# Scores of batches 3 to 7 moved into the slot ahead, in front of a double group of state products, with the PSUM banks passed on

## The chip, the cores and the metric

One core of a Trainium2 chip. TensorE (PE) multiplies matrices into PSUM, ScalarE (ACT) and VectorE (DVE) do elementwise work and empty PSUM, GpSimd (POOL) and SyncE (SP) issue most of the DMAs. The time is device microseconds of one execution of the whole kernel; lower is better.

## The reference, cut to what matters

There are 8 batches and 8 heads; x is 512 x 64 and state 32 x 64 per head. Attention runs both ways, then follow two feed-forward nets over 4352 rows (8 batches of 512 x rows and 32 state rows).

```python
scores = scale * x @ state.T             # softmax -> a;  xread = a @ state
scores2 = scale * state @ x.T            # softmax -> a2; sread = a2 @ x
h = relu(cat(xread, sread) @ w_in); y = (h * h) @ w_out
out = ((y @ w1) * (y @ w2)) @ w3 @ w_out2
```

`scores` is `scores2` transposed, so the kernel computes one of them and turns it.

## The kernel before, in words

**Stage 1, up to about 600 us, is the one that the change touches.** It computes the attention and the first feed-forward net together, for one batch c at a time, in slots. A slot i is one entry (c, f) of the list `order`: f is one of 16 blocks of 128 columns of w_in. From slot 48 on, c = i // 16 and f = i % 16; batch 2's first half, and the second halves of batches 0 to 2, stand in slots 16 to 47.

`h_tile` (L477) computes h for the slot: six full-array matmuls (L485) in fp32r, high and low words, into a bank of tag `h`. It doesn't multiply xread by w_in: as xread is a @ state, it multiplies a by the product of state and w_in, which `make_sw` has made. `act_h` (L469) then runs on ACT a Relu out of the bank (L471), a Square (L473) and the cast to the high half of `ghl` (L81), and on DVE the subtraction that gives the low half (L82). `y_tile` (L513) multiplies `ghl` by w_out with 12 full-array matmuls (L524), up to two slots later.

`make_sw` (L449) makes the state products SW of a batch and one group of four blocks: 8 matmuls in f32, each on a tile of 64 rows x 32 columns of the array, which run as 16 instructions (L454) into two banks, one per row half r. Each bank is then split: a cast on ACT (L81, `sw`) and a subtraction on DVE (L82, `sw`). `sw_pair` (L641) makes two groups one after the other, the first in the two banks of tag `m`, the second in the two of tag `h`. Pairs stand in the slots 15, 23, 31, ..., 119, directly behind the slot's `h_tile`; then follow two y tiles (24 matmuls) and no other work of TensorE.

`scores` (L315) makes the scores of one batch: 8 matmuls of the same shape as those of a state group, 16 instructions (L320), into the two `m` banks, and copies each bank to an SBUF tile `S` with ACT (L327). I call the copy of bank r S0 or S1. From `S` follow the softmax steps: `soft2` reads S directly, `soft1a` turns it on DVE (for batches from 3 on).

**PSUM** has eight banks: two `m`, two `h` and four `y`.

**What sets the order.** Lists by slot name the work beside `h_tile` and `y_tile`: `side` (behind `h_tile` and the pair) and `late` (behind `y_tile`), both kept behind an earlier slot's ghl subtraction. For batch b from 3 to 7 (BLK is 3) `att_slots` gives the attention steps for the slots from (b - 1) * 16 on, and the scores are the first of them, in slot (b - 1) * 16: 32, 48, 64, 80 and 96. Their input xT is turned on DVE (`turn_x`, L275) in slots (b - 2) * 16 + 10 and + 11. In slots 15 to 30 `conv` (L624) converts one weight block per slot; of a block of w_out, the split into high and low words (`wo`) is traced by the next slot's `conv`.

The program's order is a priority only. A planner that knows each operation's cost lays out the order of every engine ahead of the run: when an engine is free in its plan, it takes the first operation in program order that it thinks is ready, and a later one where the earlier isn't. On the chip each engine then works through its instructions in that fixed order.

**Stage 2** (from about 600 us) multiplies w3 by w_out2 and computes the second net from y. The change does not touch it.

Of the kernel before, what the change touches and what calls it, by code (L numbers as in the profile page):

```python
# [20 lines left out]
def kernel(  # L21
# [17 lines left out]
    nc = tc.nc  # L39
# [10 lines left out]
    NF = DF // P  # L50
# [6 lines left out]
    BLK = 3  # L57
# [13 lines left out]
    def bank_m(name):  # L71
        return psum.tile([P, 512], F32, tag="m", bufs=2, name=name)

    def bank_h(name):
        return psum.tile([P, 512], F32, tag="h", bufs=2, name=name)
# [4 lines left out]
    def split(hi, lo, src):  # L80
        nc.scalar.copy(hi, src)  # L81
        return nc.vector.tensor_tensor(out=lo, in0=src, in1=f32(hi), op=ALU.subtract)  # L82
# [212 lines left out]
    def att_steps(b):  # L295
# [19 lines left out]
        def scores():  # L315
            pss = [bank_m("ps_s") for _ in range(G)]
            for k in range(HG):
                for r in range(G):
                    rows = slice(r * D, (r + 1) * D)
                    nc.tensor.matmul(  # L320
                        pss[r][k * NS:(k + 1) * NS, :], stT[rows, b, k, :], xT[b, k][rows, :],
                        start=True, stop=True, tile_position=(r * D, k * NS),
                    )
            for r in range(G):
                pool, tag, bufs = (att, "S", 2) if b else (wpool, "wo", NF)
                s = pool.tile([P, 512], F32, tag=tag, bufs=bufs, name="S")
                last = nc.scalar.copy(s, pss[r])  # L327
                v["S", r] = s
            return last

# [92 lines left out]
            sread, sread_T,  # L423
        )

    def att_slots(b):
        if b >= B:
            return [[] for _ in range(NF)]
        xp, sc, s2, s1a, s1b, at, a2t, sr, srt = att_steps(b)
        if b > BLK:  # L430
            return [
                [sc], [], [s2[0], s1a[0]], [],
                [s1b[0], s2[1]], [a2t[0]], [at[0], s1a[1]], [a2t[1]],
                [s1b[1]], [sr], [at[1]], [srt], [], [], [], [],
            ]
        if b == BLK:
            return [
                [sc], [], [s2[0], s1a[0]], [], [s1b[0], s2[1]], [a2t[0]], [], [a2t[1]],
                [at[0], s1a[1]], [sr], [s1b[1]], [srt], [at[1]], [], [], [],
            ]  # L440
        return [
            [xp[0]], [xp[1]], [xp[2]], [xp[3]], [sc], [s1a[0]], [s1b[0]], [at[0], s1a[1]],
            [s1b[1]], [at[1]], [s2[0]], [a2t[0], s2[1]], [], [a2t[1]], [sr], [srt],
        ]
# [4 lines left out]
    def make_sw(b, fg, cols=slice(0, 512), banks=None):  # L449
        pss = [banks(r, "ps_sw") if banks else bank_m("ps_sw") for r in range(G)]  # L450
        for k in range(HG):
            for r in range(G):
                rows = slice(r * D, (r + 1) * D)
                mm = nc.tensor.matmul(  # L454
                    pss[r][k * NS:(k + 1) * NS, cols], stT[rows, b, k, :], win_t[fg][rows, k, cols],
                    start=True, stop=True, tile_position=(r * D, k * NS),
                )
        last_sw.append(mm)
        for r in range(G):
            if (b, fg, r) not in SW:  # L460
                SW[b, fg, r] = pa.tile([P, 2, 512], F32R, tag=f"sw{r}", bufs=2, name=f"sw{r}")
            t = SW[b, fg, r]
            split(t[:, HI, cols], t[:, LO, cols], pss[r][:, cols])
# [13 lines left out]
    def h_tile(c, f):  # L477
        ph = bank_h(f"ph{c}_{f}_")
        if c < B:
            fg, m = f // 4, f % 4  # L480
            k = 0
            for g in range(G):
                s, a = SW[c, fg, g], aT_t[c, g]
                for wi, ai in PASSES:
                    mm = nc.tensor.matmul(  # L485
                        ph, s[:, wi, m * P:(m + 1) * P], a[:, ai, :],
                        start=(k == 0), stop=(k == 3 * G - 1),
                    )
                    k += 1
            h_mms.append(mm)  # L490
            act_h(c, f, ph, 512)
        else:
            cols = slice((f % 4) * P, (f % 4 + 1) * P)
            t = pa.tile([P, 2, ND, P], F32R, tag=f"sw{f % 2}", bufs=2, name="w9")
            split(t[:, HI], t[:, LO], win_t[f // 4][:, :, cols])
            for k in range(ND):
                for i, (wi, xi) in enumerate(PASSES):
                    nc.tensor.matmul(
                        ph[:, :NT9], t[:, wi, k, :], x9_t[k // 2][:, xi, k % 2, :],
                        start=(k == 0 and i == 0), stop=(k == ND - 1 and i == 2),  # L500
                    )
            act_h(c, f, ph, NT9)
# [3 lines left out]
    def split_x9(g):  # L506
        t = pa.tile([P, 2, 2, NT9], F32R, tag=f"aT{g}", bufs=2, name="x9")
        split(t[:, HI], t[:, LO], x9T[:, 2 * g:2 * g + 2, :])
        x9_t.append(t)
# [3 lines left out]
    def y_tile(c, f):  # L513
        n = 512 if c < B else NT9
        part, (f0, f1) = [(i, sg) for i, sg in enumerate(segs[c]) if sg[0] <= f < sg[1]][0]
        if f == f0:
            for d in range(ND):
                y_ps[c, d] = bank_y(d, f"y{d}")
        if wo_t[f] is None:
            close_splits()  # L520
        t = g_t.pop((c, f))
        for d in range(ND):
            for k, (wi, gi) in enumerate(PASSES):
                nc.tensor.matmul(  # L524
                    y_ps[c, d][:, :n], wo_t[f][:, wi, d * P:(d + 1) * P], t[:, gi, :n],
                    start=(f == f0 and k == 0), stop=(f == f1 - 1 and k == 2),
                )
            if f == f1 - 1:
                pool, tag = (pa, "yo") if d < 2 or c >= B - 1 else (att, "yo2")
                o = pool.tile([P, 512], F32, tag=tag, bufs=2, name="yo")  # L530
                if d % 2 and c > 1:
                    nc.vector.tensor_copy(o[:, :n], y_ps[c, d][:, :n])
                else:
                    nc.scalar.copy(o[:, :n], y_ps[c, d][:, :n])
                nc.sync.dma_start(y_scr[c][part][:, d, :], o[:, :n])
# [49 lines left out]
    xp, sc, s2, s1a, s1b, at, a2t, sr, srt = att_steps(0)  # L585
# [12 lines left out]
    last = s1b[1]()  # L598
# [39 lines left out]
    def sw(b, fg):  # L638
        return lambda: make_sw(b, fg)

    def sw_pair(b, fg):  # L641
        make_sw(b, fg)
        make_sw(b, fg + 1, banks=lambda r, name: bank_h(name))

    side = {i: [] for i in range(NF * B)}
    late = {}
# [21 lines left out]
    pairs = {15: (2, 0), 23: (0, 2), 31: (1, 2), 39: (2, 2), 47: (3, 0)}  # L668
# [9 lines left out]
    for b in range(BLK, B):  # L678
        for i, steps in enumerate(att_slots(b)):
            late[(b - 1) * NF + i] = steps  # L680
        for g in range(G):
            i = (b - 2) * NF + 12 + g
# [17 lines left out]
    def load_wo2(i):  # L700
        t = stage["wo2", i] = w34p.tile([P, 2, 512], F32, tag="wst2", bufs=4, name="wst2")
        rows = wo2_s.rearrange("(a k p) e -> a p k e", a=4, p=NS)
        for a in range(4):
            nc.sync.dma_start(t[a * NS:(a + 1) * NS], rows[a, :, 2 * i:2 * i + 2, :])

    def split_wo2(j):
        t = w34p.tile([P, 2, DM], F32R, tag="wo2", bufs=N1, name="wo2")
        split(t[:, HI], t[:, LO], stage["wo2", j // 2][:, j % 2])
        wo2_t[j] = t

    def load_w3(kk):
        load_stage(("w3", kk), w3_s[:, 4 * kk:4 * kk + 4].rearrange("p (h d) c -> p h (d c)", h=2))
# [4 lines left out]
    for i, (c, f) in enumerate(order):  # L717
        h_tile(c, f)
        if i in pairs:
            sw_pair(*pairs[i])  # L720

        gate = done[i - 3] if i >= 8 else first
        with tc.issue_after(gate.ins):
            for job in side.get(i, ()):
                job()
        if c == B - 1 and f == 11:
            att_cm.__exit__(None, None, None)
            w34_cm = tc.tile_pool(name="w34p", bufs=1, reuse_waits="tile")
            w34p = w34_cm.__enter__()
            for j in range(N1 // 2):  # L730
                load_wo2(j)
        if c == B - 1 and f == NF - 1:
            split_x9(0)
            split_x9(1)
        if c == B:
            if f < N1:
                split_wo2(f)
            if f in (2, 4, 6, 8):
                load_w3(N1 // 2 + f // 2 - 1)
        pend.append((c, f))  # L740
        while len(pend) > (1 if i in pairs else 2):
            y_tile(*pend.pop(0))
        with tc.issue_after(done[i - 3].ins) if i >= 8 else nullcontext():
            for job in late.get(i, ()):
                job()
# [480 lines left out]
    for s, todo in enumerate((turns, turns[::-1])):  # L1226
# [9 lines left out]
        for i, (c0, c1) in enumerate(todo):  # L1236
            for m in range(QM):
                last = quad(c0, c1, m)
# [46 lines left out]
```

## Time and profile before

| | us |
|---|---|
| median of 3 runs | 1220.3 (1218.64 to 1220.49) |
| the profiled execution's own time | 1219.03 |
| its span | 1217.3 |
| PE busy in it | 1201.4 |
| DVE busy | 869.4 |
| ACT busy | 662.2 |

The span runs from the first to the last instruction of the profiled execution; its own time has 1.7 us around that. Busy time of an engine is the time in which at least one of its instructions ran. In a timeline a row merges neighbouring instructions of one kind: start, how long from the first start to the last end, and the count. Instructions on one engine overlap a little: the next starts before the one ahead has ended, so the step from start to start is what an instruction costs its engine. What stands in brackets is idle time ahead of the row and what ended it.

### The profile page before, as it was taken

How to read it: one execution, taken by the hardware profiler on the slowest of the kernel's cores; microseconds unless marked ns; L12 is line 12 of the kernel's file. 1: busy time of each engine (PE TensorE's matmuls, PEld its weight loads, DVE VectorE, ACT ScalarE, POOL GpSimd, SP SyncE). 2: the span in 40 equal slices, each digit the busy share in tenths (PEclk: the TensorE clock that was granted, in tenths of full speed). 3: DMA queues.
4: the chain of work that ended last, by engine and by line, in shares of the span. 5: the costliest groups of instructions: out<-in, count | busy, mean ns of one | idle time of the engine just before them, and what ended most of it. 6: DMA issues, size and time to landing. Idle time of an engine off the chain costs nothing.

```text
span 1217.3 us, 18891 instructions
## 1 busy us (share of the span) xinstructions
PE 1201.4 (99%) x7174; PEld 999.6 (82%) x7174; DVE 869.4 (71%) x1594; ACT 662.2 (54%) x1220; POOL 109.4 (9%) x163
## 2 busy tenths in 40 slices
PE   7999999999999999999999999999999999999998
PEld 5677777777778777778899888989898989898988
DVE  6968877677586766742435875878696957877877
ACT  6877466555464655654656653546363635453542
POOL 0000001322421121100000000000000000211110
PEclk9999999999999999999999999999999999999999
DMA  9445664835446397630413642223232540716244
GB/s 260 138 140 173 159 184 145 185 113 130 129 127 156 106 184 155 154 53 35 121 53 113 222 156 98 81 93 104 70 104 70 191 138 20 155 30 144 49 74 138
DMA packets 147922, 150.66 MB, mean 124 GB/s; under 512 B 81016, under 2 KB 107128, under 8 KB 147320
## 3 DMA queue, kind: packets, MB, share of 16 engines
q1 hardware_dynamic: 120968, 106.20, 29.6%
q0 software_dynamic: 26576, 43.00, 15.6%
q8 instruction: 56, 0.92, 0.3%
q14 instruction: 34, 0.28, 0.1%
q10 hardware_dynamic: 288, 0.26, 0.1%
HBM read 99.61 MB, written 55.05 MB: 127 GB/s over the span
## 4 chain that ended last, share of the span: by engine, by line
PE 89%; DMA 4%; DVE 3%; ACT 3%; SPq 1%; issue 0%; DVEq 0%; ACTq 0%
PE y L524 29%; PE qa L945 11%; PE qd L945 7%; PE oa L1096 5%; PE od L1096 4%; PE qc L945 4%; PE qe L945 4%; PE ps_sw L454 2%; PE ab L1006 2%; PE oe L1096 2%; PE oc L1096 2%; DMA yraw<-yscr 1%; DMA raw<-in_moe_w_in_dram 1%; PE po L1036 1%; PE ps_r L400 1%; PE ps_s L320 1%
## 5 line engine op out<-in xcount | busy, mean ns | idle before, releaser
L524 PE MATMUL y<-ghl,wo 128*128 128x512 f32 (+1 forms) x1728 | 398.9, 380 | 0.5 <-ACT ghl L81 0.5
L524 PEld LDWEIGHTS y<-ghl,wo 128*128 128x128 f32 x1728 | 310.3, 188 | 74.9 <-issue 13.4
L82 DVE TENSOR_TENSOR ghl<-r,ghl 128x512 fp32r<-128x512 f32 (+1 forms) x144 | 95.1, 660 | 163.2 <-ACT ghl L81 138.7
L953 ACT COPY s<-qa 128x512 f32<-128x512 f32 x96 | 56.5, 589 | 180.1 <-PE qa L945 179.3
L945 PE MATMUL qa<-yq,wq 128*128 128x512 f32 x576 | 143.7, 389 | 0.0
L945 PEld LDWEIGHTS qa<-yq,wq 128*128 128x128 f32 x576 | 107.7, 188 | 22.0
L945 PE MATMUL qd<-yq,wq 128*128 128x512 f32 x384 | 97.4, 389 | 0.0
L82 DVE TENSOR_TENSOR z<-q,z 128x512 fp32r<-128x512 f32 x112 | 74.3, 687 | 23.7 <-ACT z L81 23.6
L473 ACT ACTIVATE r<-r 128x512 f32<-128x512 f32 (+1 forms) x144 | 87.7, 609 | 3.2
L81 ACT CAST ghl<-r 128x512 fp32r<-128x512 f32 (+1 forms) x144 | 86.0, 597 | 3.6
L945 PEld LDWEIGHTS qd<-yq,wq 128*128 128x128 f32 x384 | 72.1, 188 | 15.0
L1136 POOL DMA_DIRECT2D out_dram<-o x24 | 28.6, 1597 | 598.2 <-DVE o L1126 598.0
L81 ACT CAST z<-q 128x512 fp32r<-128x512 f32 x112 | 68.1, 625 | 20.2 <-PE oe L1096 7.4
L957 DVE TENSOR_TENSOR s<-qa,s 128x512 f32<-128x512 f32 x32 | 22.1, 692 | 69.8 <-ACT s L953 69.8
L82 DVE TENSOR_TENSOR yq<-yraw,yq 128x512 fp32r<-128x512 f32 x98 | 64.6, 686 | 4.2 <-ACT yq L81 4.2
L81 ACT CAST yq<-yraw 128x512 fp32r<-128x512 f32 x98 | 59.3, 625 | 12.5 <-DVE yraw L874 7.6
L945 PE MATMUL qe<-yq,wq 128*128 128x512 f32 x192 | 48.7, 389 | 0.0
L945 PE MATMUL qc<-yq,wq 128*128 128x512 f32 x192 | 48.7, 389 | 0.0
L770 PE MATMUL ps_w<-wo,w3T 128*128 128x512 f32 x192 | 44.0, 390 | 0.3 <-ACT u L81 0.3
L899 DVE TENSOR_TENSOR q<-q,q 128x512 f32<-128x512 f32 x64 | 43.1, 684 | 0.0
L770 PEld LDWEIGHTS ps_w<-wo,w3T 128*128 128x128 f32 x192 | 35.9, 188 | 8.1 <-ACT u L81 0.7
L945 PEld LDWEIGHTS qc<-yq,wq 128*128 128x128 f32 x192 | 36.0, 188 | 7.5
(598 smaller groups left out, 2059.5 us busy)
## 6 DMA issues: line engine op xcount, KB each, us to landing
yraw<-yscr SPq DMA_DIRECT2D x56, 256.0 KB, 5.4
yscr<-yo SPq DMA_DIRECT2D x52, 256.0 KB, 3.1
raw<-in_moe_w_out_dram SPq DMA_DIRECT2D x16, 512.0 KB, 4.3
raw<-in_moe_w_dram POOLq DMA_DIRECT2D x64, 128.0 KB, 3.5
raw<-in_moe_w_dram POOLq DMA_DIRECT2D x16, 512.0 KB, 5.0
raw<-in_moe_w_in_dram SPq DMA_DIRECT2D x12, 512.0 KB, 4.2
out_dram<-o SPq DMA_DIRECT2D x24, 256.0 KB, 2.7
out_dram<-o POOLq DMA_DIRECT2D x24, 256.0 KB, 6.6
```

Source lines behind the costliest of these rows:

```text
L81: nc.scalar.copy(hi, src)
L82: return nc.vector.tensor_tensor(out=lo, in0=src, in1=f32(hi), op=ALU.subtract)
L454: mm = nc.tensor.matmul(pss[r][k * NS:(k + 1) * NS, cols], stT[rows, b, k, :], win_t[fg][rows, k, cols], start=True, stop=True, tile_posit ...
L473: nc.scalar.activation(r[:, :n], r[:, :n], ACTF.Square)
L524: nc.tensor.matmul(y_ps[c, d][:, :n], wo_t[f][:, wi, d * P:(d + 1) * P], t[:, gi, :n], start=(f == f0 and k == 0), stop=(f == f1 - 1 and k ...
L770: nc.tensor.matmul(ps, t[:, wi, (j % 4) * P:(j % 4 + 1) * P], wo2_t[j][:, vi, :], start=(j == 0 and k == 0), stop=(j == N1 - 1 and k == 2),)
L899: return nc.vector.tensor_tensor(out=t, in0=a, in1=b, op=ALU.subtract)
L945: nc.tensor.matmul(ps, W[w, kt][:, wi, m * P:(m + 1) * P], Y[v, kt][:, vi, :], start=(first and kt == 0 and k == 0), stop=(last and kt == ...
L953: left["copy"] = nc.scalar.copy(t, ps)
L1006: nc.tensor.matmul(pss[i][:, :NT9], w[:, wi, m * P:(m + 1) * P], Y[B, d][:, vi, :NT9], start=(d == 0 and k == 0), stop=(d == ND - 1 and k ...
L1096: nc.tensor.matmul(ps[tp][:, t % 2 * NH:(t % 2 + 1) * NH], Z[v, idx][:, vi, t * P:(t + 1) * P], rhs[:, wi], start=(first and t % 2 == 0 an ...
L1136: nc.gpsimd.dma_start(dst, src, accum_op=ALU.add)
```

## The change

The scores of batch b from 3 on leave `late` slot (b - 1) * 16. They are called in `sw_pair` of the slot before, (b - 1) * 16 - 1 (slots 31, 47, 63, 79, 95), directly in front of the two state groups. There the banks are exchanged: the scores take the two `m` banks, the first state group the two `h` banks, and the second state group the two `m` banks again, once the copies of the scores have emptied them. S1 of these batches is copied by DVE in place of ACT; S0 stays on ACT. Pairs in other slots keep their banks.

```diff
-                last = nc.scalar.copy(s, pss[r])
+                last = (nc.vector.tensor_copy if b >= BLK and r else nc.scalar.copy)(s, pss[r])
...
+    scored = {}
+
     def att_slots(b):
...
+        if b >= BLK:
+            scored[(b - 1) * NF - 1] = sc
         if b > BLK:
             return [
-                [sc], [], [s2[0], s1a[0]], [],
+                [], [], [s2[0], s1a[0]], [],
...
         if b == BLK:
             return [
-                [sc], [], [s2[0], s1a[0]], [], [s1b[0], s2[1]], [a2t[0]], [], [a2t[1]],
+                [], [], [s2[0], s1a[0]], [], [s1b[0], s2[1]], [a2t[0]], [], [a2t[1]],
...
-    def sw_pair(b, fg):
-        make_sw(b, fg)
-        make_sw(b, fg + 1, banks=lambda r, name: bank_h(name))
+    def sw_pair(b, fg, sc=None):
+        banks = [None, lambda r, name: bank_h(name)]
+        if sc:
+            sc()
+            banks.reverse()
+        for n in range(2):
+            make_sw(b, fg + n, banks=banks[n])
...
-            sw_pair(*pairs[i])
+            sw_pair(*pairs[i], scored.get(i))
```

## Rows read from the trace of the kernel before

**Rows 1.** The page: span, TensorE's busy time, its granted clock by slices.

```profile
span 1217.3 us, 18891 instructions
...
PE 1201.4 (99%) x7174; PEld 999.6 (82%) x7174; DVE 869.4 (71%) x1594; ACT 662.2 (54%) x1220; POOL 109.4 (9%) x163
...
PEclk9999999999999999999999999999999999999999
```

**Rows 2.** Timeline of PE, slots 95 to 98: start us, us, engine, line, operation, count.

```profile
469.50 1.95 PE L454 MATMUL ps_sw<-win,stT 64*32 64x512 f32 x32
471.37 5.73 PE L524 MATMUL y<-ghl,wo 128*128 128x512 f32 x24
476.94 1.52 PE L485 MATMUL ph__4934<-aT,sw 128*128 128x512 f32 x6
478.40 1.09 PE L320 MATMUL ps_s<-xT,stT 64*32 64x512 f32 x16
479.42 1.65 PE L485 MATMUL ph__4970<-aT,sw 128*128 128x512 f32 x6
...
483.64 1.52 PE L485 MATMUL ph__5007<-aT,sw 128*128 128x512 f32 x6
```

**Rows 3.** Timeline of PE from pair to second tile, slots 111 to 114, no scores.

```profile
542.58 1.95 PE L454 MATMUL ps_sw<-win,stT 64*32 64x512 f32 x32
...
555.47 1.52 PE L485 MATMUL ph__5649<-aT,sw 128*128 128x512 f32 x6
```

**Rows 4.** Timeline of PE: eight instructions of one row half, 256 columns.

```profile
27.51 0.64 PE L454 MATMUL ps_sw<-win,stT 64*32 64x256 f32 x8 [1.78 <-ACT xT L313]
```

**Rows 5.** Timeline of ACT, slots 95 and 96.

```profile
469.60 0.60 ACT L471 ACTIVATE r<-ph__4863 128x512 f32<-128x512 f32 x1 [2.16 <-PE ph__4863 L485]
470.23 0.63 ACT L473 ACTIVATE r<-r 128x512 f32<-128x512 f32 x1
470.90 0.62 ACT L81 CAST ghl<-r 128x512 fp32r<-128x512 f32 x1
471.42 2.04 ACT L81 CAST sw<-ps_sw 128x512 fp32r<-128x512 f32 x4
...
480.32 1.07 ACT L327 COPY S<-ps_s 128x512 f32<-128x512 f32 x2
```

**Rows 6.** Timeline of DVE, slot 95.

```profile
471.55 0.69 DVE L82 TENSOR_TENSOR ghl<-r,ghl 128x512 fp32r<-128x512 f32 x1 [3.38 <-PE ps_sw L454]
472.15 1.28 DVE L82 TENSOR_TENSOR sw<-ps_sw,sw 128x512 fp32r<-128x512 f32 x2
```

**Rows 7.** One line's instructions: duration ns min/median/max, first and last start us.

```profile
L532 DVE COPY yo<-y x16: 419/684/692, 154.0 to 670.9; 128x512 f32<-128x512 f32 x14, 128x256 f32<-128x256 f32 x2
```

**Rows 8.** Timelines of ACT and DVE, slot 23.

```profile
143.64 0.62 ACT L81 CAST ghl<-r 128x512 fp32r<-128x512 f32 x1
144.23 0.62 ACT L81 CAST wo<-cw 128x512 fp32r<-128x512 f32 x1
144.75 2.04 ACT L81 CAST sw<-ps_sw 128x512 fp32r<-128x512 f32 x4
...
143.50 0.69 DVE L152 CUSTOM_DVE_ANT_0 cw<-raw,cw 128x1024 uint16<-128x1024 uint16 x1
```

**Rows 9.** Timelines of PE and DVE, slot 15: a bank released late.

```profile
104.59 2.48 PE L454 MATMUL ps_sw<-win,stT 64*32 64x512 f32 x32
106.99 5.28 PE L524 MATMUL y<-ghl,wo 128*128 128x512 f32 x22
...
104.38 0.68 DVE L82 TENSOR_TENSOR aT<-ps_a,aT 128x512 fp32r<-128x512 f32 x1
```

**Rows 10.** Timeline of DVE: the last turn of scores' input before slot 95.

```profile
456.04 0.71 DVE L279 STREAM_TRANSPOSE xT<-xb 128x512 f32<-128x512 f32 x1
```

**Rows 11.** Timeline of PE in the early slots.

```profile
57.05 1.89 PE L524 MATMUL y<-ghl,wo 128*128 128x512 f32 x7
58.93 1.16 PE L454 MATMUL ps_sw<-win,stT 64*32 64x512 f32 x16
```

## The prediction

> **What bounds the kernel now.** I read the page first. TensorE (PE) is busy 1201.4 of 1217.3 us, and the clock that it was granted reads 9 tenths or more in all 40 slices, the upper of its two levels (2.4 GHz) [rows 1]. So only what shortens or lengthens TensorE's own stream counts, and ScalarE (ACT) and VectorE (DVE) count only where TensorE waits for one of their results.
>
> Then the timeline of PE around one place that the change touches, the end of slot 95 (scores of batch 7; the other four, after slots 31, 47, 63 and 79, repeat it). In slot 95 a double group of state products stands: 32 instructions on 64x32 tiles, start 469.50, next work at 471.37, so 1.87 us. One slot later the scores stand alone: 16 instructions of the same shape, 478.40 to 479.42, so 1.02 us, where half of a double group would be 0.94 [rows 2]. From the start of the pair to the h tile of slot 98 it is 483.64 - 469.50 = 14.14 us. Slots 111 to 114 hold the same work without scores: 555.47 - 542.58 = 12.89 us [rows 2, 3]. So one batch's scores cost 1.25 us of TensorE. A second group behind a first one adds 1.87 - 1.02 = 0.85 us. The other 0.40 us is what one entry into the small tiles and back costs, seen as slower neighbours and a first fill.
>
> **The change, part by part.**
>
> 1. The scores join the pair. One entry less per batch: -0.40 us, five batches, -2.0 us. This is all that the change can give on TensorE, since the instructions are the same; the gain ends there.
>
> 2. The scores go a slot earlier. Their input xT is turned on DVE for the last time at 456.04 + 0.71 = 456.75, and they would start at 469.50 [rows 2, 10]: 12.7 us of margin, no wait. They issue no DMA, and no DMA queue is passed.
>
> 3. The banks. Before, the pair's first group used the two m banks and its second the two h banks. Now the scores take m, the first state group h, the second state group m again, and so it has to wait until both S copies have emptied m. I count from the first small tile, t = 0 (469.50 in the trace). The scores are through at 1.02. The first state group starts at 0.85 and needs the bank of the tile just computed: its Relu runs from 0.10 to 0.70 [rows 5], so it is free in time, nothing. The second state group would start at 2 x 0.85 = 1.70.
>
> 4. The S copies, by the order of their queues. ACT goes through Relu, Square and the ghl cast (469.60, 470.23, 470.90), and the next ACT instruction starts at 471.42, t = 1.92 [rows 5]. In the slot of the scores the S copies already stood behind that cast (480.32, that is 1.92 after the scores' 478.40 too). So S0 runs from 1.92 to about 2.46 (two took 1.07). S1 is now a DVE copy; no S copy on DVE is in this trace, and the nearest row is the yo copy from a bank, 0.684 us [rows 7]. Where it stands on DVE decides. The subtraction that makes the low half of ghl starts at 471.55 (t = 2.05), its successor at 472.15 (t = 2.65) [rows 6]. If S1 is behind it: 2.65 + 0.68 = 3.33. If S1 is ahead of it (DVE was idle before): 1.02 + 0.06 + 0.68 = 1.76. If one more operation of weight conversion of the longest kind slips in, 0.69 [rows 8]: about 4.0.
>
>    I take 3.33, for this reason. The order on each engine is fixed by a planner that picks what it thinks is ready. In slot 23 it put the cast wo ahead of the sw casts on ACT, though wo belongs to a job of the next slot, and its own input was only being finished at 143.50 + 0.69 = 144.19 [rows 8]. The first group of a pair stands directly behind an h tile, as the scores will, and is through on the chip about 1 us after its start [rows 2], before the ghl cast even begins (t = 1.40) [rows 5]. So the planner believed that a small-tile group ends later than the ghl cast does. For the scores, in the same place and of the same shape, it will believe the same: when the ghl subtraction becomes ready in its plan, S1 is not, and S1 comes behind. For the same reason it will see no wait ahead of the second state group (it thinks that the first is still running), and will leave the three groups together.
>
>    What a late bank then costs is in the trace once: in slot 15 a DVE subtraction held an m bank until 104.38 + 0.68 = 105.06, the pair began at 104.59 and took 106.99 - 104.59 = 2.40 us in place of 1.87. So 0.53 lost for a bank 0.47 late: 0.06 to pass on the signal, the rest in full, and nothing was put between [rows 9].
>
>    So the second state group starts at 3.33 + 0.06 = 3.39 in place of 1.70: 1.69 us of waiting per batch. The bounds of this term are 1.76 + 0.06 - 1.70, about 0.1 (both copies at once), and 4.0 + 0.06 - 1.70, about 2.4.
>
>    Two rules of the Trainium skill bear on this. "TensorEngine Tiling (Array Packing)", section PSUM Bottleneck, says that tiling speeds up TensorE but not the emptying of PSUM, and advises both ScalarE and VectorE for it. By the durations alone (0.59 and 0.68 against 0.85 per group) that advice would do, and the term would be the 0.1 of the lower bound; the rows on the queues speak against it here. "PSUM — Partial Sum Buffer", section Engine vs sequencer instructions, says that the queues of ScalarE and VectorE are strictly first in, first out; by that rule an S1 behind the subtraction cannot pass it, and the sum is the one below.
>
> 5. What is queued behind the waiting group: in order on TensorE, 24 y matmuls and the next h tiles, all 1.69 us later. Nothing of it can be caught up, as TensorE has next to no idle time [rows 1].
>
> 6. The copies themselves: five ACT copies of about 0.55 us go, five DVE copies of 0.68 us come. Covered: the casts and subtractions of the pair behind them (0.5 to 0.65 us each) are next needed by the h tile of slot 96, which has 24 y matmuls in front of it, 471.37 to 476.94 [rows 2], and would start at t = 7.44 + 0.85 + 1.69 = 9.98. The two subtractions of the first state group would end at about 3.33 + 1.28 = 4.6 [rows 6]. Without that cover each batch would lose up to the 0.68 us of the added copy. Nothing taken.
>
> 7. The scores' place one slot later falls empty; softmax steps get S earlier, and nothing on TensorE waits for them there. Nothing.
>
> The sum: 5 x (1.69 - 0.40) = +6.45 us. The profiled execution took 1219.03 us (span 1217.3): 1225.5. The median of the runs is 1220.3, 1.27 above it, so 1226.7 us for the median.
>
> **Rivals.**
>
> A. S1 ahead of the ghl subtraction. For it: DVE stood idle for 3.38 us before that subtraction [rows 6]. Against: the wo row. Then S0 is last: 2.46 + 0.06 - 1.70 = 0.82 of waiting, net +0.42 a batch, +2.1 us: 1222.4. Chance 0.15.
>
> B. Not slower: the planner sees the wait, and pulls y matmuls in front of the second state group, as it put seven of a y tile's twelve matmuls ahead of a lone state group in the early slots [rows 11]. Then TensorE enters the small tiles twice per batch, as before, and never waits: 0.0, so 1220.3. It decides where the planner believes that the first state group ends before the copies do; slot 23 speaks against. Chance 0.15. A worse form, 0.05: only the row half whose bank is free goes first and y comes between the halves. Eight instructions of one half took 0.64 us for 256 columns, so a half saves no time [rows 4], and each batch pays about 0.85 more than before: +4.3, 1224.6.
>
> C. Both copies run as soon as they could: S0 between Square and the cast, 1.36 to 1.95 by the ACT rows, S1 at once. Waiting 0.3, net -0.1 a batch, -0.5 us; at the very best, no wait at all, -2.0 us: 1219.8 to 1218.3. For it: nothing but idle DVE. Against: in the scores' slot the S copies stood behind the cast. Chance 0.10.
>
> **How the numbers follow.** My forecast (S1 behind the subtraction) has 0.55, A 0.15, B 0.20 with its worse form, C 0.10. Its own range is 1225 to 1229.5: one conversion operation more in front of S1 in some batches adds up to 0.7 a batch. The whole range reaches down to take in B and half of C: 1219.4 to 1229.5; under 2 in 10 stay outside. Within 0.2% means 2.4 us, about what a measurement of this kernel can tell from no change. Slower: the forecast and B's worse form, 0.60. Same: A, B's main form and most of C, 0.35. Faster: 0.05, since even the whole gain of 2.0 us is less than that bound.
>
> **What would show it.** In the changed kernel each of the five places should have 48 small-tile instructions in one piece, about 4.4 us long in place of the 2.7 that three groups need (bounds: 2.8 and 5.1), its wait put down to DVE's S copy; the S copy on DVE should start right behind a ghl subtraction; and the slot behind should show two h tiles side by side, as slots 112 and 113 do. If the S copy stands in front of the subtraction, A is right; if y stands between the groups, B; if the piece lasts 2.8 us, C. The sum is also wrong if the clock falls in the waits: an idle stretch of 1.78 us ahead of 27.51 left its slice at 9 [rows 1, 4].

## The result, and the profile after

The changed kernel took 1227.21 us (median of 6 runs, 1225.21 to 1227.57), the kernel before 1219.91 us (6 runs, 1217.48 to 1220.49). The ratio is 1.0061 (95% interval 1.0048 to 1.0074), so the change costs 5.9 to 9.0 us. The forecast was 1226.7 us, slower by 6.4 us.

The page of the changed kernel, for [rows 1]:

```profile
span 1225.5 us, 18896 instructions
...
PE 1206.2 (98%) x7174; PEld 1002.2 (82%) x7174; DVE 869.7 (71%) x1599; ACT 660.2 (54%) x1215; POOL 109.7 (9%) x163
...
PEclk8999999999999999999999999999999999999999
```

The span grew by 8.2 us, TensorE's busy time by 4.8 us. Of its granted clock, the first slice now reads 8.

The place behind slot 63, on PE (start us, us, engine, line, operation, count, idle time ahead and its end), for [rows 2]:

```profile
327.90 1.09 PE L320 MATMUL ps_s<-xT,stT 64*32 64x512 f32 x16
328.78 1.06 PE L458 MATMUL ps_sw<-win,stT 64*32 64x512 f32 x16
330.45 1.93 PE L458 MATMUL ps_sw<-win,stT 64*32 64x512 f32 x16 [0.61 <-ACT S L327]
332.31 5.73 PE L528 MATMUL y<-ghl,wo 128*128 128x512 f32 x24
```

The three groups stand in one piece, 327.90 to 332.31, which is 4.41 us; between the second and the third TensorE is idle. The weight loads of the same place show on what, since a load waits where its matmul would:

```profile
328.65 0.28 PEld L458 LDWEIGHTS ps_sw<-win,stT 64*32 64x32 f32 x15 [0.19 <-ACT r L475]
330.45 0.13 PEld L458 LDWEIGHTS ps_sw<-win,stT 64*32 64x32 f32 x2 [1.51 <-ACT S L327]
331.29 0.18 PEld L458 LDWEIGHTS ps_sw<-win,stT 64*32 64x32 f32 x14 [0.71 <-DVE S L327]
```

Two loads of the third group go at 330.45, the other 14 only at 331.29, when DVE's copy of S has ended. The queues of ACT and DVE there, for [rows 5, 6]:

```profile
329.29 0.62 ACT L81 CAST ghl<-r 128x512 fp32r<-128x512 f32 x1
329.82 0.58 ACT L327 COPY S<-ps_s 128x512 f32<-128x512 f32 x1
...
329.94 0.69 DVE L82 TENSOR_TENSOR ghl<-r,ghl 128x512 fp32r<-128x512 f32 x1 [3.38 <-PE ps_sw L458]
330.55 0.68 DVE L327 COPY S<-ps_s 128x512 f32<-128x512 f32 x1
```

Counted from 327.90, S0 ends at 2.50, and S1 stands behind the ghl subtraction and ends at 3.33. The loads follow 0.06 us later. Over all five places, the view of the copies' line says who waited:

```profile
L327 DVE COPY S<-ps_s x5: 682/683/709, 181.6 to 479.3; 128x512 f32<-128x512 f32 x5
...
who waited for it (us, times):
  PEld ps_sw L458: 11.2, 10
  PE ps_sw L458: 3.6, 5
```

What one place costs is read from the start of the h tile in the slot with the pair to that of the next slot that the change touches, 16 slots on. Slots 79 to 95 of the kernel before and of the changed kernel:

```profile
394.96 1.52 PE L485 MATMUL ph__4163<-aT,sw 128*128 128x512 f32 x6
...
468.05 1.52 PE L485 MATMUL ph__4863<-aT,sw 128*128 128x512 f32 x6
```

```profile
400.80 1.52 PE L489 MATMUL ph__4163<-aT,sw 128*128 128x512 f32 x6
...
475.18 1.52 PE L489 MATMUL ph__4863<-aT,sw 128*128 128x512 f32 x6
```

Before it is 468.05 - 394.96 = 73.09 us, after it 475.18 - 400.80 = 74.38 us: +1.29. Read in the same way, the five places (slots 31, 47, 63, 79, 95) cost 1.34, 1.27, 1.27, 1.29 and 1.27 us, together 6.44 us.

The two profiles differ by more, 1227.48 - 1219.03 = 8.45 us. The changed kernel's was already 1.96 us late at slot 31, before the first edited place, and TensorE won back 0.3 us between 660 and 750 us; the other 0.35 us lies behind TensorE's last matmul and outside the span. The early stretches by engine (busy us and count each, then the granted clock, DMA share and GB/s), of the kernel before and of the changed kernel:

```profile
15.00:20.00 5.00, 4.04 (x24) 2.91 (x24) 4.63 (x12) 3.31 (x7) 0.00 (x0) 0.70 0.89 171
20.00:25.00 5.00, 4.07 (x21) 3.23 (x20) 2.87 (x6) 3.56 (x8) 0.00 (x0) 0.96 0.73 196
```

```profile
15.00:20.00 5.00, 4.00 (x24) 3.06 (x24) 4.67 (x12) 3.11 (x7) 0.00 (x0) 0.66 0.84 161
20.00:25.00 5.00, 4.40 (x13) 3.20 (x13) 2.89 (x7) 2.90 (x6) 0.00 (x0) 0.50 0.74 203
```

In the changed kernel's profile TensorE ran from 20 to 25 us at the lower of its two levels (0.50 is 1.2 GHz), in the other almost wholly at the upper. Up to slot 31 TensorE has the same 1071 matmuls in both kernels. The second profile of the kernel before, below, tells whether this belongs to the change.

### The profile page after: what moved, and what is told of

Its sections match the earlier page's. It is cut to its first block, busy times and chain, and to the rows that moved or that the text cites. A ratio compares the mean times of both kernels' runs of the same rounds, so it can differ in the third digit from the quotient of the medians.

```text
span 1225.5 us, 18896 instructions
## 1 busy us (share of the span) xinstructions
PE 1206.2 (98%) x7174; PEld 1002.2 (82%) x7174; DVE 869.7 (71%) x1599; ACT 660.2 (54%) x1215; POOL 109.7 (9%) x163
## 4 chain that ended last, share of the span: by engine, by line
PE 87%; DMA 4%; ACT 4%; DVE 4%; issue 1%; SPq 1%; DVEq 0%; ACTq 0%
PE y L528 28%; PE qa L953 10%; PE qd L953 7%; PE oa L1104 5%; PE od L1104 4%; PE qc L953 4%; PE qe L953 4%; PE ps_sw L458 2%; PE ab L1014 2%; PE oe L1104 2%; PE oc L1104 2%; DMA yraw<-yscr 1%; PE po L1044 1%; DMA raw<-in_moe_w_in_dram 1%; PE ps_r L400 1%; ACT r L475 1%
## 5 line engine op out<-in xcount | busy, mean ns | idle before, releaser
L458 PE MATMUL ps_sw<-win,stT 64*32 64x512 f32 (+1 forms) x528 | 39.6, 583 | 8.7 <-ACT S L327 3.6
```

The lines of the kernel that those rows point to most:

```text
L458: mm = nc.tensor.matmul(pss[r][k * NS:(k + 1) * NS, cols], stT[rows, b, k, :], win_t[fg][rows, k, cols], start=True, stop=True, tile_posit ...
```

## The experiments

Each median stands beside runs of the kernel before: 1219.91 us for the changed kernel (6 runs), 1219.31 us for the next four kernels (22 runs), 1219.16 us for the last three (21 runs); each kernel itself ran 4 to 11 times. The ratio and its interval are estimated from all these runs, so a ratio differs a little from the quotient of two medians. t counts from a place's first small tile. "Place" is the cost of one by the starts of the h tiles, slots 63 to 79.

| kernel | S0 ends, t | S1 ends, t | piece us | place us | median us | ratio to before |
|---|---|---|---|---|---|---|
| changed | 2.50 | 3.33 | 4.41 | +1.27 | 1227.21 | 1.0061 (1.0048 to 1.0074) |
| S1 on ACT | 2.50 | 2.98 | 4.06 | +0.92 | 1224.46 | 1.0044 (1.0031 to 1.0057) |
| S1 ahead | 2.50 | 1.91 | 3.58 | +0.44 | 1223.02 | 1.0029 (1.0017 to 1.0040) |
| both ahead | 1.76 | 1.91 | 2.98 | -0.02 | 1221.15 | 1.0012 (1.0003 to 1.0021) |
| y between | 2.50 | 3.33 | two pieces | 0.00 | 1220.77 | 1.0016 (1.0008 to 1.0025) |
| S1 copied twice | 2.50 | 4.27 | 5.44 | +2.30 | 1232.44 | 1.0110 (1.0095 to 1.0126) |
| before, S1 on DVE | - | - | - | 0.00 | 1220.15 | 1.0004 (0.9995 to 1.0012) |
| both ahead, not batch 3 | 1.77 | 1.91 | 2.98 | 0.00 | 1219.18 | 1.0000 (0.9991 to 1.0009) |

**S1 back on ACT.**

```diff
-                last = (nc.vector.tensor_copy if b >= BLK and r else nc.scalar.copy)(s, pss[r])
+                last = nc.scalar.copy(s, pss[r])
```

> The changed kernel with S1 back on ACT behind S0; everything else as changed. My theory (the second state group waits for the copy that empties its bank last): by the ACT rows of the kernel before, S0 ends about 2.5 us and S1 about 3.0 us after the first small tile, so the wait falls from 1.69 to about 1.35 us per place, the piece of three groups lasts about 4.1 us in place of 4.4, and the kernel is 4.8 us slower than before (ratio 1.004), 1.6 us faster than the changed one. Rival (the loss is the copy on DVE holding up the ghl and sw subtractions, not the bank): with no copy on DVE the loss is gone, ratio 0.9985 to 1.000. Rival (the loss comes from the moved scores, whatever the copies do): as the changed kernel, ratio 1.006.

Measured: ratio 1.0044, the place +0.92 (expected +0.95), the piece 4.06 us (expected about 4.1). PE, then ACT, behind slot 79:

```profile
401.60 1.09 PE L320 MATMUL ps_s<-xT,stT 64*32 64x512 f32 x16
...
404.15 1.57 PE L458 MATMUL ps_sw<-win,stT 64*32 64x512 f32 x16 [0.60 <-ACT S L327]
405.66 3.70 PE L528 MATMUL y<-ghl,wo 128*128 128x512 f32 x15
...
403.52 1.06 ACT L327 COPY S<-ps_s 128x512 f32<-128x512 f32 x2
```

Both copies are through at 403.52 + 1.06 = 404.58, t = 2.98, and y starts 1.08 us later, at 405.66. The loss shrank with the wait, which the second rival doesn't allow, and stayed without the DVE copy, which the first doesn't allow: both fall. (The two ratios' intervals overlap; the places, 0.92 against 1.27 us, tell the two kernels apart.)

**S1 ahead of the ghl subtraction.** `front()`, which is left out here, issues the scores inside `act_h` in the five slots; `issue_after` puts the subtraction behind the copy.

```diff
...
-        done.append(split(t[:, HI, :n], t[:, LO, :n], r[:, :n]))
+        nc.scalar.copy(t[:, HI, :n], r[:, :n])
+        b = front()
+        with tc.issue_after(copies[b, 1].ins) if b else nullcontext():
+            done.append(nc.vector.tensor_tensor(out=t[:, LO, :n], in0=r[:, :n], in1=f32(t[:, HI, :n]), op=ALU.subtract))
...
```

> The changed kernel with the ghl subtraction of the five slots queued behind S1 on DVE; S0 stays behind the ghl cast on ACT. My theory: S1 is through at about 1.8 us, S0 at 2.5 us after the first small tile, so S0 ends the wait, 0.85 us per place; the piece lasts about 3.6 us; 5 x (0.85 - 0.40) = +2.3 us against before (ratio 1.002). Rival (DVE copy holding up the subtractions): the subtraction comes no earlier than in the changed kernel, so ratio 1.006. Rival (moved scores as such): 1.006.

Measured: ratio 1.0029, the place +0.44, the piece 3.58 us. PE, ACT and DVE behind slot 79:

```profile
399.30 1.09 PE L322 MATMUL ps_s<-xT,stT 64*32 64x512 f32 x16
...
401.85 1.09 PE L461 MATMUL ps_sw<-win,stT 64*32 64x512 f32 x16 [0.60 <-ACT S L329]
402.88 5.29 PE L541 MATMUL y<-ghl,wo 128*128 128x512 f32 x22
...
401.22 0.58 ACT L329 COPY S<-ps_s 128x512 f32<-128x512 f32 x1
...
400.52 0.69 DVE L329 COPY S<-ps_s 128x512 f32<-128x512 f32 x1 [2.56 <-PE ps_s L322]
```

S1 is through at 1.91, S0 at 2.50, and the third group now starts 0.05 us behind S0 (401.85). The four places from slot 47 on cost 0.44 to 0.45 each, as expected; slot 31 cost 1.46. There weight conversion kept DVE busy, S1 ended only at t = 3.51, behind S0 (3.02), and the piece lasted 4.58 us. The five places make 3.2 us in place of 2.3, within the ratio's interval (2.1 to 4.9 us).

**Both copies at once.**

```diff
...
         nc.scalar.activation(r[:, :n], ph[:, :n], ACTF.Relu)
         t = pa.tile([P, 2, 512], F32R, tag="ghl", bufs=3, name="ghl")
-        nc.scalar.activation(r[:, :n], r[:, :n], ACTF.Square)
-        done.append(split(t[:, HI, :n], t[:, LO, :n], r[:, :n]))
+        b = front()
+        with tc.issue_after(copies[b, 0].ins) if b else nullcontext():
+            nc.scalar.activation(r[:, :n], r[:, :n], ACTF.Square)
+            with tc.issue_after(copies[b, 1].ins) if b else nullcontext():
+                done.append(split(t[:, HI, :n], t[:, LO, :n], r[:, :n]))
...
```

> The changed kernel with both copies at once: on ACT, Square and the ghl cast of the five slots queued behind S0 (right behind Relu), on DVE the ghl subtraction behind S1. My theory: both copies end 1.7 to 1.8 us after the first small tile, just when the second state group would start, so the wait is 0 to 0.1 us, the piece lasts 2.7 to 2.8 us and only the saved entry is left: 5 x (0.0 to 0.1 - 0.40) = -1.5 to -2.0 us against before (ratio 0.9985). ghl is 0.6 us later, which is covered, as its y tile comes some 10 us later. Rival (moved scores as such, or anything but the two banks): still slower than before, ratio 1.003 to 1.006.

Measured: ratio 1.0012, so my expectation of a gain missed by about 3 us, and the rival's 1.003 was missed too. PE, ACT and DVE behind slot 79:

```profile
398.77 1.09 PE L322 MATMUL ps_s<-xT,stT 64*32 64x512 f32 x16
...
401.75 5.75 PE L541 MATMUL y<-ghl,wo 128*128 128x512 f32 x24
...
399.94 0.59 ACT L329 COPY S<-ps_s 128x512 f32<-128x512 f32 x1 [0.48 <-PE ps_s L322]
...
399.99 0.69 DVE L329 COPY S<-ps_s 128x512 f32<-128x512 f32 x1 [2.56 <-PE ps_s L322]
```

The copies start 1.17 and 1.22 us after the first small tile, not at 1.08, and DVE's ends at 1.91. The third group's loads for S1's bank can't go before that, and y starts at 2.98 where three groups without a wait need 2.72 (1.87 for two and 0.85 for one more). That leaves a gain of 3.12 - 2.98 = 0.14 a place, with 3.12 us the price of a pair (1.87) and lone scores (1.25) in the kernel before. Slots 79 and 95 gave 0.13 and 0.14; slots 47 and 63 gave 0.0. Their pieces are as short (2.99 us), but three slots on, in slots 50 and 66, a y tile waits 0.27 and 0.26 us for a bank that ACT's yo copy empties, and the gain is gone. PE's weight loads, then ACT, in slot 50:

```profile
267.98 2.14 PEld L541 LDWEIGHTS y<-ghl,wo 128*128 128x128 f32 x10 [0.27 <-ACT yo L551]
...
267.35 0.57 ACT L551 COPY yo<-y 128x512 f32<-128x512 f32 x1
```

In the kernel before, the two yo copies there (264.47 and 265.46) stood ahead of the softmax's multiply (265.94). With S a slot earlier, the multiply (263.53) and an exp (264.16) stand ahead of a Relu, and the yo copies come behind. So the scores' earlier place is not free for ACT's queue; in the changed kernel, whose wait is longer, no y tile waits there.

Slot 31 lost 1.40 us. ACT, then DVE, there:

```profile
179.79 0.62 ACT L81 CAST wo<-cw 128x512 fp32r<-128x512 f32 x1 [1.15 <-DVE cw L152]
180.32 0.58 ACT L329 COPY S<-ps_s 128x512 f32<-128x512 f32 x1
...
180.74 0.68 DVE L329 COPY S<-ps_s 128x512 f32<-128x512 f32 x1
```

The planner had put work of the weight conversion in front of both copies: on ACT the wo cast, which waited for its own input, and on DVE a step (L149) from 180.13 on. S0 ends at t = 2.96, S1 at 3.49, so it is S1 that sets the end of this piece (4.56 us, 1.07 behind it).

**y between the groups.**

```diff
         for n in range(2):
             make_sw(b, fg + n, banks=banks[n])
+            if sc and n == 0:
+                y_tile(*pend.pop(0))
```

> The changed kernel with the first of the two y tiles (12 matmuls, 2.7 us) between the first and the second state group of the five places; copies as in the changed kernel. My theory: the copies end (3.4 us) before the second state group's turn (1.9 + 2.8 = 4.7 us), no wait; two entries into the small tiles per batch, as before the change: 0.0 us against before (ratio 1.000, within 0.5 us). This prices the entry: if an entry cost nothing, the time would be the same too, but then the kernel with both copies at once would not be below 1.000. Rival (moved scores as such): ratio 1.006.

Measured: ratio 1.0016, not 1.000. PE behind slot 47:

```profile
252.05 1.09 PE L320 MATMUL ps_s<-xT,stT 64*32 64x512 f32 x16
252.93 1.06 PE L458 MATMUL ps_sw<-win,stT 64*32 64x512 f32 x16
253.92 3.01 PE L528 MATMUL y<-ghl,wo 128*128 128x512 f32 x12
256.87 1.09 PE L458 MATMUL ps_sw<-win,stT 64*32 64x512 f32 x16
257.88 3.03 PE L528 MATMUL y<-ghl,wo 128*128 128x512 f32 x12
```

No wait is left, and the places behind slots 47 to 95 cost 0.01 us or less each, as expected: two entries into the small tiles, as before the change. What the profile has on top stands elsewhere: slot 31's place cost 1.08 us, for the y tile behind the h tile of slot 34 had to wait 0.48 us, and its weight loads another 0.47 us, for yo copies late in ACT's queue:

```profile
193.85 3.35 PE L528 MATMUL y<-ghl,wo 128*128 128x512 f32 x12 [0.48 <-ACT yo L538]
```

The ratio's interval (1.0 to 3.0 us more than before) just holds these 1.1 us.

**S1 copied twice.**

```diff
+                if b >= BLK and r:
+                    nc.vector.tensor_copy(s, pss[r])
                 last = (nc.vector.tensor_copy if b >= BLK and r else nc.scalar.copy)(s, pss[r])
```

> The changed kernel with the bank of S1 read twice by DVE (the same copy, done two times), so that the bank comes free later; the output is unchanged. In the order laid out, a weight conversion step of 0.34 us stands between the two copies. My theory: the bank is free 0.60 + 0.34 = 0.94 us later, TensorE waits that much longer in each of the five places, so +1.27 + 0.94 = 2.2 us a place, 11.1 us against before (ratio 1.009). Rival (DVE time as such, or the moved scores): five DVE operations off TensorE's path, as the changed kernel, ratio 1.006.

Measured: ratio 1.0110, the place +2.30. PE and DVE behind slot 79:

```profile
404.03 1.09 PE L320 MATMUL ps_s<-xT,stT 64*32 64x512 f32 x16
...
406.59 1.04 PE L460 MATMUL ps_sw<-win,stT 64*32 64x512 f32 x2 [0.61 <-ACT S L329]
408.45 1.09 PE L460 MATMUL ps_sw<-win,stT 64*32 64x512 f32 x14 [0.83 <-DVE S L329]
409.47 2.79 PE L530 MATMUL y<-ghl,wo 128*128 128x512 f32 x11
...
406.69 0.68 DVE L328 COPY S<-ps_s 128x512 f32<-128x512 f32 x1
407.29 0.42 DVE L135 TENSOR_SCALAR raw<-raw 128x512 int32<-128x512 uint32 x1
407.62 0.68 DVE L329 COPY S<-ps_s 128x512 f32<-128x512 f32 x1
```

The second copy ends at 408.30, t = 4.27, so 0.94 us later than in the changed kernel, as expected; the other 14 matmuls start 0.15 us behind it, and the place costs 1.03 us more than in the changed kernel. So DVE's copy of S1 sets the end of the piece almost one for one. The ratio lies above the 1.009 expected: slot 31 cost 2.59 and the other four places 2.3 each, in place of 2.2. Together that is 11.8 us, which the interval (11.6 to 15.4 us) just holds.

**S1 on DVE alone, scores where they were.** The first line of the change, on the kernel before.

> The kernel before with S1 of batches 3 to 7 copied by DVE, scores and banks where they were. My theory: no matmul waits for those banks there, so 0.0 us (ratio 1.000). Rival (the copy on DVE is the cost in the changed kernel): ratio 1.003 to 1.006.

Measured: ratio 1.0004, no difference. Where no matmul waits for the bank, the copy on DVE costs nothing.

**The kernel before, profiled again.**

> The kernel before, unchanged, for a second profile. The changed kernel's profile was 1.96 us late before the first edited place, with the half clock granted until about 26 us. My theory (this varies from run to run and does not belong to the change): the first h tile after 29 us, and with it slot 15, lies between 103.0 and 105.0 us, not at 103.02 again. Rival (the change causes it): slot 15 at 103.0 again.

Measured: 1219.44 us; slot 15 began at 103.90 us, against 103.02 and, in the changed kernel, 104.98. The early stretches:

```profile
15.00:20.00 5.00, 4.01 (x21) 2.90 (x22) 4.27 (x12) 2.57 (x6) 0.00 (x0) 0.50 0.89 161
20.00:25.00 5.00, 4.29 (x19) 3.34 (x20) 2.87 (x6) 3.59 (x8) 0.00 (x0) 0.85 0.70 187
```

In this profile of the same kernel the clock was at the lower level from 15 to 20 us and rose before 25. Over the eight other profiles slot 15 began between 103.49 and 104.98, the changed kernel with the latest. So the start varies by 0.9 us between two profiles of one kernel, and by up to 2.0 us over kernels that differ only behind it; the kernel before with S1 on DVE was 1.72 us late there too. The first profile of the kernel before was the earliest of all.

**Both copies at once, batch 3 as before the change.**

```diff
-        if b >= BLK:
+        if b > BLK:
             scored[(b - 1) * NF - 1] = sc
```

(and the same bound for the DVE copy; batch 3 keeps its scores in slot 32)

> The kernel with both copies at once, but batch 3 left as before the change (in its slot weight conversion stood ahead of S0 and cost 1.4 us). My theory, from the profile of the kernel with both copies at once: S0 ends 1.76 us after the first small tile, the third group loses 0.25 us and saves 0.40 us, four places: -0.6 us against before (ratio 0.9995, within the noise), 1.7 us faster than with batch 3 included. Rival (something else in the moved scores costs): ratio 1.001, as with batch 3 included.

Measured: ratio 1.0000, as fast as the kernel before, and 1.5 us faster than with batch 3 by the ratios, whose intervals overlap; in the profiles slot 31's place costs 0.00 in place of 1.40 us. In the profile its four places gave -0.01, 0.00, +0.15 and +0.15 us, a gain of 0.3 us together, half of what was expected, that the median can't tell from nothing; slots 50 and 66 have the same waits for a yo copy (0.28 us in slot 50). That batch 3 cost the kernel its gain is borne out, though what ended last in slot 31 was DVE's S1 and not S0. It is the best of the versions tried, and no improvement that could be shown.

## Why the prediction was right

**The saved entry** was put at 0.40 us a batch. The places agree with it and the wait taken together: changed kernel, S1 on ACT, S1 ahead and S1 copied twice all cost the piece less 3.12 us (4.41, 4.06, 3.58 and 5.44 give 1.29, 0.94, 0.46 and 2.32; measured 1.27, 0.92, 0.44 and 2.30). The 0.40 by itself rests on the rows of the kernel before: in no run did a third group go without a wait, and the most that a place gave was 0.15 us.

**The place of S1 on DVE** was the choice that decided, and it was read from one row of another slot: a cast of lower priority put ahead of the sw casts [rows 8]. In the changed kernel S1 stood behind the ghl subtraction in all five places, and the groups were left in one piece. What the planner believes of a group's end is an inference that no run tests; what is shown is the order that it laid out. With S1 forced ahead the loss fell to a third, as rival A had it.

**The wait** was put at 1.69 us a place, from 3.33 us for S1's end and 0.06 us to pass it on; the trace has 3.33 and 0.06 (the two matmuls that go ahead, once S0's bank is free, gain nothing). Together with the entry: +1.29 forecast, +1.27 to 1.34 measured, 6.44 us in sum against 6.45.

**Nothing is caught up in stage 1**: the profile of the changed kernel is 8.40 us late at slot 111 (1.96 from the start and 6.44 from the five places) and 8.40 at slot 127. Between 660 and 750 us TensorE wins back 0.3 us. The prediction had ruled that out; but the second profile of the kernel before wins 0.5 us there with no edit, and S1 on ACT 1.5 us, so this stretch varies and can't be put down to the change.

**Where it was off**: by the ratio the median moved about 0.9 us more than the sum. The interval holds the sum, and the start, which no place of the change touches, varies by about as much between two profiles of one kernel. That nothing on TensorE waits where the softmax steps get S earlier held in the changed kernel and in the others with a long wait; with the wait short or gone, the yo copies behind those steps came late (slots 34, 50 and 66). Rival C's price of -0.1 us a place was about right (0.0 to -0.15 with both copies at once, slot 31 aside), but its best case, no wait at all, cannot be had with these two copies: they start only 1.17 and 1.22 us after the first small tile. My expectation for that run leaned on the best case, left out the weight conversion in slot 31, and missed.

The runs give a rule for this kernel: the piece ends 1.08 us after the last copy of S (0.06 to pass it on and 1.02 for the group; 1.17 where the bank was read twice), in slot 31 too. So the change breaks even where that copy ends at 3.12 - 1.08 = 2.04 us. By the same sum it would gain all of its 0.40 only below 2.72 - 1.08 = 1.64, which no run reached.

## What to carry to other kernels

Before three producers are put in a row over the banks of two, add up where the copies that empty the first pair stand in the queues of their engines, not how long they take: here 0.68 us of copying was through only 3.33 us after the start, because the engine's order put an earlier tile's work ahead. A saving of one setup (0.4 us) is small against one place in such a queue (0.6 us). Work that is moved earlier also pulls along what depends on it: here the softmax steps passed the yo copies in ACT's queue, which showed only once the larger wait was gone. Where a planner lays out the order, look in the trace for one case in which it let something pass ahead, infer from it what it believes to be slow, and check the order in the next trace.

## What the runs showed of the hardware that I had not expected

The clock granted to TensorE in the first 30 us differs from run to run of one program: at the lower level from 15 to 20 us in one profile of the kernel before, 0.70 of full in the same stretch of the other, and at the lower level from 20 to 25 us in the changed kernel's. In the first and the last of these three everything behind came 0.9 and 2.0 us later, up to a third of the effect looked for. That the clock is the whole of it is not shown: with both copies at once it reads 1.00 from 15 to 20 us and 0.66 from 20 to 25, as much low time in all as in the first profile (0.70 and 0.96), and slot 15 still began 0.97 us later. Comparing stretches that begin behind the start took it out.
